# Order edges in the first stage of an attention and mixture kernel, one sink transposition per unit, and later splits of the first expert's weights

## The chip, the cores and the metric

The program runs on one core of a Trainium2 chip. The core has a matrix engine (PE, with weight loads listed apart as PEld), a vector engine (DVE), a scalar engine (ACT), a general engine (POOL), and a queue of transfers that the sync engine (SP) issues. Each engine takes its instructions in the order in which the program lists them. The metric is the time of one execution in microseconds on the device; smaller is better.

## The reference, cut to what matters

```
scores = q @ k.T / sqrt(64)           # 4 batches, 8 heads, 768 positions, head 64
keep   = (position < 4) | (0 <= distance < 128)     # 4 sinks and a window of 128
a      = softmax(where(keep, scores, -1e9));  x = (a @ v) as [3072, 512]
h      = max(x @ w1, x @ w2, x @ w3);  x = h @ w_out          # first mixture, ff 768
order the 3072*8 gate logits, fill 8 experts with 384 tokens each
out[tokens of e] = relu(x[tokens] @ u1[e]) @ u2[e]            # second mixture, ff 1024
```

## The kernel before

The tokens are cut into eight groups of 384 (half a sequence each). The attention of a group is four units, one per pair of heads, 32 units in all, counted by `u['n']`. A unit is loaded (`load`), prepared (`prep`), scored (`score`: six products into banks of the pool `pss`, which has three, copied and masked into the tile T by DVE and ACT), put through the softmax (`soft`: maximum `m` on DVE, six exponentials on ACT with their sums in `l`, the reciprocal on DVE, and the multiplication of T on POOL, line 154) and multiplied with the values (`pv`). In `pv` PE transposes T: three transpositions of blocks of 128 columns into the bank `pt`, of which only the eight rows of the four sinks of two heads are kept, and three for each head into the bank `pp`. ACT and DVE copy the sink rows from `pt` as a high and a low part into the tile `psb` (lines 160 and 161), which meets the sinks' values (tile `vk`, written on POOL in lines 108 and 109) in one product per head, line 177 or 190. The first eight units and units 10 and 11 use the values as they were loaded ("native"); the others split all operands into a high and a low part.

The result of unit p of a group is x_p, a quarter of the contraction of the first mixture. `group` multiplies it with the three weights (line 293, twelve products to a bank of the pool `mm`, which has two banks), so a bank can only be finished when all four units of its group have delivered. The first group's results go straight into a high and a low part (`split`, lines 28 and 29).

The weights of the first mixture arrive as 64-bit words. `single` loads a block (line 228; a ring of four places in the tile HL), takes bits from the second words into a bank of `pss` on DVE (line 235), scales the first words on ACT (line 236), joins both on DVE (line 237) and adds on POOL (line 238). Then a copy on ACT (line 220) and a difference on POOL (line 221) make the high and low parts. A ring place is free for the next load after the addition.

The order of all this up to the last group is worked out when the program is built, by a scheduler that runs a timeline of its own and takes instructions by priority; each engine then follows its list. An edge added by hand (`add_manual_dep`) fixes the order of two instructions without a semaphore where both stand on one engine.

After the last group the tokens are given to experts round by round (lines 418 to 549, mostly on DVE with short counting products on PE), while PE multiplies the last groups with w_out (`x2`, line 318, and `by_rows`, line 350). In the last call of `x2` each bank is copied by ACT (line 320) and split twice (`keep`: ACT line 324, DVE line 325). The experts follow (`expert`): per expert eight blocks f of u1 and u2 are loaded (lines 561 and 562, three places each), split by `weights` (ACT line 566, then DVE or POOL line 567, six places) and multiplied (lines 622 and 615).

Of the kernel before, what the change touches and what calls it, by code (L numbers as in the profile page):

```python
# [21 lines left out]
NEG=-8.0e9  # L22
# [2 lines left out]
    nc.tensor.transpose(out,x,f32(ident))  # L25

def split(nc,hl,x):
    nc.scalar.activation(hl[0],x,AF.Copy)
    nc.vector.tensor_tensor(hl[1],x,f32(hl[0]),op=OP.subtract)

class Attn:
    def __init__(s, tc, q,k,v,vs, keep, consts, pst, psp, pss, psv, work):
        s.tc=tc; s.nc=nc=tc.nc; s.q,s.k,s.v,s.vs=q,k,v,vs
        s.pst,s.psp,s.pss,s.psv,s.w=pst,psp,pss,psv,work
        jp=work.tile([128,128],I32,name="jp",tag="qs0",bufs=2)
        nc.gpsimd.iota(jp,pattern=[[1,128]],base=0,channel_multiplier=-1)
        s.ident=keep.tile([128,128],FR,name="ident")
        nc.vector.tensor_scalar(s.ident,jp,0.0,None,op0=OP.is_equal)
        s.ca=consts.tile([128,2,128],U8,name="ca")
        nc.vector.tensor_scalar(s.ca[:,0,:],jp,0.0,None,op0=OP.is_le)  # L40
        nc.vector.tensor_scalar(s.ca[:,1,:],jp,0.0,None,op0=OP.is_gt)
        s.ul=consts.tile([128,2,128],BF,name="ul")
        nc.vector.tensor_scalar(s.ul[:,0,:],jp,0.0,None,op0=OP.is_lt)
# [10 lines left out]
        s.behind=None; s.n=0; s.no=('kh0','kh1')  # L54
# [9 lines left out]
    def load(s,b,hf,p,native=False):  # L64
        nc=s.nc; w=s.w
        nb=3+hf; S=768; D=64
        u=dict(b=b,hf=hf,p=p,nb=nb,n=s.n,nat=native); s.n+=1
        i=(b*2+hf)*4+p
        half=[(slice(64*h,64*h+64),slice(64-64*h,128-64*h)) for h in range(2)]

        if native:
            u['KK']=s.kf[u['n']%len(s.kf)] if u['n']<8 else s.zeros([s.two(u,[128,4,132],FT,f"kh{h}") for h in range(2)])
            for h,(a,o) in enumerate(half): nc.sync.dma_start(u['KK'][h][a,:nb],s.k[i,a,:nb*132].rearrange("d (c j) -> d c j",j=132))
            u['QF']=w.tile([128,384],FT,name="qf",tag="qs0",bufs=2)
            nc.sync.dma_start(u['QF'],s.q[i])
            u['vn']=w.tile([128,4,2,64],FT,name="vnn",tag="vsp")
        else:
            u['kn']=w.tile([128,4,132],FT,name="kn",bufs=1)
            ld=[nc.sync.dma_start(u['kn'][:,:nb],s.k[i,:,:nb*132].rearrange("p (c j) -> p c j",j=132))]
            u['qn']=[w.tile([128,384],FT,name=f"qn{h}",bufs=1) for h in range(2)]  # L80
            ld+=[nc.sync.dma_start(u['qn'][h][r],s.q[i,a]) for h,(a,o) in enumerate(half) for r in (a,o)]
            if s.behind is not None:
                for x in ld: s.tc.add_manual_dep(x.ins,s.behind.ins.name,mybir.DependencyInfo(mybir.DependencyClass.NoSync,mybir.DependencyReason.DATA),reason="order of loads")
                s.behind=None
            u['vn']=w.tile([128,4,2,64],FT,name="vn",bufs=1)
        nc.sync.dma_start(u['vn'][:,:nb],s.v[i].rearrange("t (c h d) -> t c h d",h=2,d=64)[:,:nb])
        u['sv']=w.tile([40,2,64],FT,name="vns",bufs=1)
        nc.sync.dma_start(u['sv'],s.vs[b*4+p].rearrange("r (h d) -> r h d",h=2))
        return u
    def prep(s,u):  # L90
# [16 lines left out]
        hi,lo=(bass.AP(tensor=VK.tensor,offset=VK.offset+o,ap=[[VK.ap[0][0],40],[st,2],[1,64]]) for o,st in (((0,64),(128,64)) if nat else ((0,192),(64,64))))  # L107
# [37 lines left out]
    def soft(s,u):  # L145
        nc=s.nc; w=s.w; T=u['T']
        m=w.tile([128,6],FT,name="m"); l=w.tile([128,6],FT,name="l")
        nc.vector.tensor_reduce(m,T,axis=AX.X,op=OP.max)
        nc.scalar.activation(m,m,AF.Copy,scale=-0.125)
        for j in range(6):  # L150
            nc.scalar.activation(T[:,j,:],T[:,j,:],AF.Exp,scale=0.125,bias=m[:,j:j+1],accum_out=l[:,j:j+1])
        nc.scalar.activation(l,l,AF.Copy,bias=1e-9)
        nc.vector.reciprocal(l,l)  # L153
        nc.gpsimd.tensor_tensor(T,T,l[:,:,None].to_broadcast([128,6,132]),op=OP.mult)  # L154
    def pv(s,u,x):
        nc=s.nc; w=s.w; T=u['T'].rearrange('p u j -> p (u j)'); hf=u['hf']; nb=u['nb']; nat=u['nat']
        psk=s.pst.tile([128,512],FT,name="pt")
        for i in range(3): flip(nc,psk[:,i*128:(i+1)*128],T[:,264*i+128:264*i+256],s.ident)
        PB=s.pb[u['n']%2]
        nc.scalar.activation(PB[0:8],psk[0:8,:384],AF.Copy)  # L160
        nc.vector.tensor_tensor(PB[32:40],psk[0:8,:384],f32(PB[0:8]),op=OP.subtract)
        jobs=[]
        if hf: jobs.append((0,128,0,0))
        for i in range(3): jobs.append((i*256+128,256 if i<2 else 128,i*128,i+hf))
        for h in range(2):
# [8 lines left out]
            if nat:  # L174
                if h==0:
                    po=s.psv.tile([128,512],FT,name="po")
                    for a_ in range(2): nc.tensor.matmul(po[:,:384],u['VK'][:,a_,:],PB,start=(a_==0),stop=False,skip_group_check=True)
                for c,n,q,blk in jobs:
                    nc.tensor.matmul(po[a,q:q+n],u['vn'][:,blk,h,:],Af[:,c:c+n],start=False,stop=True,skip_group_check=True)  # L179
                if h==1:  # L180
                    for c in x: split(nc,c,po[:,:384]) if type(c) is tuple else nc.scalar.activation(c,po[:,:384],AF.Copy)
# [29 lines left out]
class Moe1:  # L211
# [10 lines left out]
    def single(s,src,ring=False):  # L222

        nc=s.nc
# [9 lines left out]
        s.n+=1  # L234
        nc.vector.tensor_scalar(A,st[:,:,1],0x07ffffff,3,op0=OP.bitwise_and,op1=OP.logical_shift_left)
        nc.scalar.activation(C,st[:,:,0].bitcast(U32),AF.Copy,scale=2.0**-29)
# [70 lines left out]
    def x2(s,H,t0,LG,x2d,n=260,pool=None,keep=None):  # L307

        nc=s.nc; main=s.main; mms=[]
        for t in range(3):  # L310
            o=pool.tile([128,512],FT,name="xq",bufs=4) if pool else s.room(t).tile([128,520],FT,name="xo",bufs=1)
            for u in range(2):
# [6 lines left out]
                with s.tc.high_priority():  # L319
                    nc.scalar.activation(o[:,u*n:(u+1)*n],ps[:,0:n],AF.Copy)  # L320
                    if keep is not None:
                        for d in (2*u,2*u+1):
                            h,l=keep(t,d); c=ps[:,(d-2*u)*128:(d-2*u)*128+128]
                            nc.scalar.activation(h,c,AF.Copy)
# [227 lines left out]
class Moe2:  # L552
# [5 lines left out]
    def weights(s,ev,f):  # L558
# [79 lines left out]
def attention_mixtures(tc,q,k,v,vs,words,wg,u1,u2,out,off=60,spread=(0,1,3,4),native=8,order='a0 a0 a0 a0 w a1 w a1 w a1 w a1 w w a2',order1='a2 o o o o o o a2 a2',back=1,at=(1,0),s1=300,s2=400,nring=6):  # L638
    nc=tc.nc
    PS=bass.MemoryType.PSUM  # L640
    with ExitStack() as ctx:
# [116 lines left out]
def layout(np, i):  # L758
# [12 lines left out]
    vs = np.zeros((4, 4, 40, 2, 64), v.dtype)  # L771
    for h in range(2):
        for r in range(2):
            vs[:, :, 32*r+4*h:32*r+4*h+4, h] = v[:, :, h, :4]
# [30 lines left out]
```

## Time and profile before

| | |
|---|---|
| median of three timed runs | 972.17 us (970.58 to 973.03) |
| the profiled execution, its own time | 963.85 us |
| its span, first to last instruction | 962.1 us |
| mean granted clock of TensorE | 0.992 |
| PE busy | 926.6 us of the span |

The profile shows one execution. Its own time is 1.75 us above its span. The differences that matter for a change are read inside its span and then set against the median of the timed runs, which is 8.3 us above it. A row of a timeline gives the start in us from the span's start, the busy time, the engine, the line, what is written from what, and in brackets the idle time of the engine just before, with what released it. Neighbouring equal rows are merged with their count (x3).

### The profile page before, as it was taken

To read this page: it belongs to the slowest core of one execution; us is meant where nothing else is said; L and a number is where in the kernel's file an instruction comes from. 1 tells how busy PE (TensorE), PEld (TensorE's weight loads), DVE (VectorE), ACT (ScalarE), POOL (GpSimd) and SP (SyncE) were. 2 spreads that over 40 slices of the span, in tenths; PEclk is the share of its full clock that TensorE was granted. 3 is DMA by queue.
4 is the path that set the end of the run, shared out by engine and by line. 5 is a ranking of instruction groups with operands and counts; after the bars stand their busy time and mean duration, and the time that the engine had idled before them with its cause. 6 is when DMAs were issued, how large, how long until landed. Compare 5 with 4: busy or idle time off the path is not lost.

```text
span 962.1 us, 18532 instructions
## 1 busy us (share of the span) xinstructions
PE 926.6 (96%) x6552; PEld 848.2 (88%) x6552; DVE 712.3 (74%) x1855; ACT 489.4 (51%) x1341; POOL 263.8 (27%) x271
## 2 busy tenths in 40 slices
PE   5899999999999999999999999999999999999996
PEld 4679899979989999999999998888888888888895
DVE  6777887677998997886755445888989889874320
ACT  4477554776777876685653211334434434344431
POOL 3687535131232222221311000011103022054321
PEclk8999999999999999999999999999999999999999
DMA  7465321331212222122210002544345353454420
GB/s 212 134 217 165 105 79 62 106 123 49 69 58 90 66 71 71 56 66 80 66 53 2 1 1 88 184 152 132 111 155 176 100 168 119 151 194 164 136 68 33
DMA packets 54444, 99.36 MB, mean 103 GB/s; under 512 B 7792, under 2 KB 24688, under 8 KB 54352
## 3 DMA queue, kind: packets, MB, share of 16 engines
q1 hardware_dynamic: 44464, 75.90, 25.5%
q0 software_dynamic: 3840, 12.45, 3.6%
q10 hardware_dynamic: 6048, 9.83, 2.8%
q8 instruction: 51, 0.84, 0.3%
q14 instruction: 41, 0.34, 0.1%
HBM read 82.17 MB, written 16.12 MB: 102 GB/s over the span
## 4 chain that ended last, share of the span: by engine, by line
PE 73%; DVE 11%; issue 6%; DMA 4%; ACT 3%; POOL 2%; POOLq 0%; SPq 0%; DVEq 0%; ACTq 0%
PE mm L293 25%; PE mm L622 12%; PE acc L615 12%; PE mm L318 6%; PE rc L420 3%; PE po L189 3%; PE ps L130 2%; PE pt L25 2%; PE po L179 2%; DVE kh_w L102 2%; PE pp L25 1%; DMA qf<-in_q_dram 1%; DVE L L185 1%; PE acc L350 1%; PE ps L132 1%
## 5 line engine op out<-in xcount | busy, mean ns | idle before, releaser
L615 PE MATMUL acc<-wbh,HL 128*128 128x512 f32 x384 | 133.1, 401 | 0.0
L318 PE MATMUL mm<-woh,HL 128*128 128x260 f32 (+1 forms) x432 | 88.2, 292 | 5.1 <-ACT xo L320 3.9
L296 DVE TENSOR_TENSOR hm<-mm,hm 128x384 f32<-128x384 f32 x96 | 53.1, 554 | 53.1 <-PE mm L293 48.0
L566 ACT ACTIVATE wah<-sa 128x512 fp32r<-128x512 f32 x64 | 40.5, 632 | 83.5 <-PE mm L622 68.1
L615 PEld LDWEIGHTS acc<-wbh,HL 128*128 128x128 f32 x384 | 71.4, 188 | 12.6 <-ACT HL L625 0.4
L318 PEld LDWEIGHTS mm<-woh,HL 128*128 128x128 f32 x432 | 69.5, 190 | 8.4 <-ACT xo L320 4.8
L566 ACT ACTIVATE wbh<-sb 128x512 fp32r<-128x512 f32 x64 | 40.4, 631 | 71.4 <-PE acc L615 68.7
L615 PE MATMUL acc<-wbl,HL 128*128 128x512 f32 x192 | 76.5, 398 | 0.0
L634 POOL DMA_INDIRECT out_dram<-og,idx x24 | 29.2, 1218 | 169.1 <-ACT og L633 166.3
L293 PE MATMUL mm<-xh,w1h 128*128 128x384 f32 x192 | 66.6, 347 | 1.4 <-ACT w1h L220 0.5
L622 PE MATMUL mm<-HL,wah 128*128 128x384 f32 x256 | 67.4, 341 | 0.0
L293 PE MATMUL mm<-xh,w0h 128*128 128x384 f32 x192 | 66.1, 344 | 0.9 <-DVE hm L296 0.7
L293 PE MATMUL mm<-xh,w2h 128*128 128x384 f32 x192 | 66.4, 346 | 0.0
L293 PE MATMUL mm<-xh,w0l 128*128 128x384 f32 x192 | 65.1, 339 | 0.4 <-POOL w0l L221 0.4
L567 DVE TENSOR_TENSOR wbl<-sb,wbh 128x512 fp32r<-128x512 f32 x64 | 45.2, 706 | 27.1 <-ACT wbh L566 26.8
L293 PE MATMUL mm<-xh,w2l 128*128 128x384 f32 x192 | 65.2, 340 | 0.0
L293 PE MATMUL mm<-xl,w2h 128*128 128x384 f32 x192 | 64.9, 338 | 0.0
L293 PE MATMUL mm<-xh,w1l 128*128 128x384 f32 x192 | 64.9, 338 | 0.0
L293 PE MATMUL mm<-xl,w0h 128*128 128x384 f32 x192 | 64.8, 338 | 0.0
L293 PE MATMUL mm<-xl,w1h 128*128 128x384 f32 x192 | 64.8, 338 | 0.0
L626 DVE SCALAR_TENSOR_TENSOR HL<-mm,HL 128x384 fp32r<-128x384 f32 x64 | 35.5, 555 | 37.8 <-ACT HL L625 37.6
L154 POOL TENSOR_TENSOR T_w<-T_w,l 128x792 f32<-128x792 f32 x22 | 34.2, 1552 | 106.6 <-DVE l L153 106.5
(331 smaller groups left out, 2829.3 us busy)
## 6 DMA issues: line engine op xcount, KB each, us to landing
sa<-in_u_dram SPq DMA_DIRECT2D x64, 256.0 KB
sb<-in_u_dram SPq DMA_DIRECT2D x64, 256.0 KB
HL<-in_words_dram SPq DMA_DIRECT2D x18, 512.0 KB
qn<-in_q_dram SPq DMA_DIRECT2D x88, 96.0 KB
x2d<-xo ACTq DMA_DIRECT2D x15, 256.0 KB
kn<-in_k_dram SPq DMA_DIRECT2D x12, 264.0 KB
st<-in_words_dram SPq DMA_DIRECT2D x6, 512.0 KB
vn<-in_v_dram SPq DMA_DIRECT2D x12, 256.0 KB
```

Of the source, the lines that this page charges most:

```text
L25: nc.tensor.transpose(out,x,f32(ident))
L154: nc.gpsimd.tensor_tensor(T,T,l[:,:,None].to_broadcast([128,6,132]),op=OP.mult)
L189: nc.tensor.matmul(po[:,q:q+n],u['VS'][:,blk,128*h:128*h+128],part[:,c:c+n],start=(part is H and j==0),stop=False,skip_group_check=True)
L293: nc.tensor.matmul(ps[:,:384],s.W[i][a][:,p,f*128:(f+1)*128],X[p][b],start=(n==0),stop=(n==11)); n+=1
L296: else: nc.vector.tensor_tensor(m,ps[:,:384],m,op=OP.max)
L318: mms.append(nc.tensor.matmul(ps[:,:n],H[f][a][:,t*128:(t+1)*128],s.WO[b][:,f,u,c],start=(k==0),stop=(k==17))); k+=1
L566: nc.scalar.activation(h,src,AF.Copy)
L567: (nc.gpsimd if s.n>=6 and nm=="wa" else nc.vector).tensor_tensor(l,src,f32(h),op=OP.subtract)
L615: s.mms.append(nc.tensor.matmul(acc[t],H[f][a][:,t*128:(t+1)*128],W[f][1][b],start=(f==0 and n==0),stop=(f==F-1 and n==2))); n+=1
L622: s.mms.append(nc.tensor.matmul(ps[:,:384],W[f][0][a][:,k,:],X[k][b],start=(n==0),stop=(n==11))); n+=1
L626: nc.vector.scalar_tensor_tensor(l,ps[:,:384],0.0,f32(h),op0=OP.max,op1=OP.subtract)
L634: st=nc.gpsimd.indirect_dma_start(out=s.out,out_offset=bass.IndirectOffsetOnAxis(ap=idx[:,t:t+1],axis=0),in_=o,in_offset=None)
```

## The change

`follow(tc,i,j)` places instruction i behind instruction j. In the first stage it puts the first two scalings of weight words (line 236) behind the softmax sums of unit 0, the next two behind the last exponential of unit 1, and the first DVE steps of three blocks behind the maxima of units 1 and 2; it puts the split of x_0 behind the sums of unit 2, and the clearing of unit 3's T behind the multiplication of unit 1. The DVE product of the first three blocks goes to a bank of `mm` in place of one of `pss`. From unit 8 on, POOL copies the 24 sink columns of T into a small tile S, PE transposes that once, ACT and DVE copy 24 rows of 128 columns where they copied eight rows of 384, and POOL spreads them over `psb` with a mask; the tile of the sinks' values gets 56 rows in place of 40. In the second mixture the splits of blocks f = 4 and above of the first expert are placed on ACT behind the last split of `x2`.

```diff
+def follow(tc,i,j):
+    tc.add_manual_dep(i.ins,j.ins.name,mybir.DependencyInfo(mybir.DependencyClass.NoSync,mybir.DependencyReason.DATA),reason="order on an engine")
...
+        jq=work.tile([128,3],I32,name="jq",tag="m",bufs=2)
+        nc.gpsimd.iota(jq,pattern=[[-8,3]],base=0,channel_multiplier=1)
+        nc.vector.tensor_scalar(jq,jq,-40,None,op0=OP.bitwise_and)
+        s.sm=consts.tile([128,3],FT,name="sm"); nc.vector.tensor_scalar(s.sm,jq,0.0,None,op0=OP.is_equal)
+        s.us=consts.tile([128,128],FR,name="us"); nc.vector.memset(f32(s.us),0.0)
...
-        u['sv']=w.tile([40,2,64],FT,name="vns",bufs=1)
+        u['sv']=w.tile([56,2,64],FT,name="vns",bufs=1)
...
-        if hf==0: nc.gpsimd.memset(T[:,0:2,:],NEG)
+        if hf==0:
+            z=nc.gpsimd.memset(T[:,0:2,:],NEG)
+            if u['n']==3: follow(s.tc,z,s.ev['s',1])
...
+        z=s.ev['l',u['n']]=nc.scalar.activation(l,l,AF.Copy,bias=1e-9)
+        if u['n']==2: follow(s.tc,s.ev['x',0],z)
...
+        if u['n']>=8:
+            S=u["S"]=w.tile([128,24],FT,name="S",bufs=1)
+            nc.gpsimd.tensor_copy(S.rearrange("p (i e) -> p i e",e=8),T.rearrange('p (i v) j -> p i (v j)',v=2)[:,:,128:136])
...
+            U=s.us
+            flip(nc,psk[0:24,0:128],u['S'],s.ident)
+            nc.scalar.activation(U[0:24],psk[0:24,:128],AF.Copy)
+            nc.vector.tensor_tensor(U[32:56],psk[0:24,:128],f32(U[0:24]),op=OP.subtract)
+            nc.gpsimd.tensor_tensor(PB[0:56].rearrange("r (i q) -> r i q",q=128),f32(U)[0:56,None,:].to_broadcast([56,3,128]),s.sm[0:56,:,None].to_broadcast([56,3,128]),op=OP.mult)
...
-        A=s.pss.tile([128,512],FT,name="ps").bitcast(I32); C=st[:,:,0]
+        A=(s.mm.tile([128,512],FT,name="mm") if ring and s.n<3 else s.pss.tile([128,512],FT,name="ps")).bitcast(I32); C=st[:,:,0]
...
+        if n<4: follow(s.tc,z,s.ev['l',0] if n<2 else s.ev['e',1])
+        if n<3: follow(s.tc,y,s.ev['m',1 if n<1 else 2])
...
-            nc.scalar.activation(h,src,AF.Copy)
+            z=nc.scalar.activation(h,src,AF.Copy)
+            if s.n==0 and f>=4: follow(s.tc,z,s.final)
```

## Rows read from the trace of the kernel before

**Rows 1.** The page: busy time of each engine, share of the span, instructions.
```profile
PE 926.6 (96%) x6552; PEld 848.2 (88%) x6552; DVE 712.3 (74%) x1855; ACT 489.4 (51%) x1341; POOL 263.8 (27%) x271
```

**Rows 2.** Stretches of the span: start:end, length, busy us (count) per engine, clock, DMA.
```profile
0.00:20.00 20.00, 10.80 (x39) 7.57 (x40) 13.45 (x53) 6.78 (x24) 8.27 (x21) 0.97 0.75 223
...
20.00:40.00 20.00, 16.01 (x77) 10.61 (x76) 15.62 (x36) 9.27 (x37) 8.85 (x12) 0.86 0.37 105
...
40.00:60.00 20.00, 18.10 (x94) 13.80 (x93) 15.77 (x33) 15.82 (x56) 16.65 (x16) 1.00 0.59 195
...
300.00:400.00 100.00, 99.13 (x676) 98.06 (x676) 88.10 (x166) 70.62 (x224) 26.23 (x29) 1.00 0.24 68
```

**Rows 3.** Timeline of ACT, 12 to 28 us: start, busy us, instruction, [idle before <-releaser].
```profile
12.38 0.66 ACT L236 ACTIVATE HL<-HL 128x512 int32<-128x512 uint32 x1 [9.87 <-DMA HL<-in_words_dram]
...
16.76 0.65 ACT L236 ACTIVATE HL<-HL 128x512 int32<-128x512 uint32 x1 [1.09 <-DMA HL<-in_words_dram]
...
17.31 0.19 ACT L152 ACTIVATE l<-l 128x6 f32<-128x6 f32 x1
...
27.46 0.49 ACT L28 ACTIVATE xh<-po 128x384 fp32r<-128x384 f32 x1 [2.08 <-PE po L179]
```

**Rows 4.** Timeline of PE, the first 50 us.
```profile
4.76 4.55 PE L130 MATMUL ps<-woh,qf 128*128 128x132 f32 x14 [4.76 <-POOL wol L57]
...
18.25 0.68 PE L130 MATMUL ps<-wol,qf 128*128 128x260 f32 x2 [2.41 <-DVE wol L142]
...
22.34 2.09 PE L130 MATMUL ps<-woh,qf 128*128 128x132 f32 x6 [1.43 <-DMA qf<-in_q_dram]
...
49.83 0.55 PE L25 MATMUL pp<-ident,T_w 128*128 128x128 f32 x3 [1.86 <-DVE A_w L170]
```

**Rows 5.** Timeline of POOL near 25 us.
```profile
25.19 0.32 POOL L121 MEMSET T_w<- 128x264 f32 x1 [5.88 <-PE pp L25]
```

**Rows 6.** Timeline of DVE, 30 to 56 us.
```profile
30.18 0.69 DVE L235 TENSOR_SCALAR ps<-HL 128x512 int32<-128x512 int32 x1
...
37.73 0.97 DVE L148 TENSOR_REDUCE m<-T_w 128x6 f32<-128x792 f32 x1
...
55.70 0.56 DVE L29 TENSOR_TENSOR xl<-po,xh 128x384 fp32r<-128x384 f32 x1 [0.41 <-ACT xh L28]
```

**Rows 7.** The stretch from 20 to 25 us, columns as in rows 2.
```profile
20.00:25.00 5.00, 3.57 (x15) 2.90 (x14) 2.67 (x5) 4.91 (x25) 0.00 (x0) 0.50 0.56 132
```

**Rows 8.** Timeline of PE at 57 us: two sets of three transpositions.
```profile
57.12 0.49 PE L25 MATMUL pt<-ident,T_w 128*128 128x128 f32 x3
57.44 0.49 PE L25 MATMUL pp<-ident,T_w 128*128 128x128 f32 x3
```

**Rows 9.** Timeline of ACT, DVE and PE, 625 to 646 us.
```profile
625.61 0.63 ACT L566 ACTIVATE wah<-sa 128x512 fp32r<-128x512 f32 x1 [2.26 <-DMA sa<-in_u_dram]
...
626.15 0.26 ACT L324 ACTIVATE HL<-mm 128x128 fp32r<-128x128 f32 x1
...
626.44 0.29 DVE L325 TENSOR_TENSOR HL<-mm,HL 128x128 fp32r<-128x128 f32 x1 [2.02 <-ACT HL L324]
...
626.79 0.39 PE L318 MATMUL mm<-woh,hh 128*128 128x256 f32 x1 [1.78 <-DVE HL L325]
...
645.91 0.42 PE L622 MATMUL mm<-xh,wah 128*128 128x384 f32 x1
```

**Rows 10.** Timeline of one later unit, 256 to 265 us, all engines.
```profile
256.27 0.48 ACT L160 ACTIVATE psb<-pt 8x384 fp32r<-8x384 f32 x1
...
258.16 0.28 POOL L108 CAST vk<-vns 40x128 fp32r<-40x128 f32 x1 [5.64 <-PE po L190]
...
259.18 0.55 DVE L161 TENSOR_TENSOR psb<-pt,psb 8x384 fp32r<-8x384 f32 x1
...
260.37 1.02 POOL L116 TENSOR_TENSOR vsp<-vn,vsp 128x384 fp32r<-128x384 f32 x1 [1.93 <-ACT vsp L115]
...
264.82 0.39 PE L190 MATMUL po<-psb,vk 128*128 128x384 f32 x1
```

**Rows 11.** Line 102 on DVE: count, shortest/median/longest ns, first and last start.
```profile
L102 DVE TENSOR_TENSOR kh_w<-kn,kh_w x24: 565/704/4530, 95.4 to 436.2; 64x396 fp32r<-64x396 f32 x12, 64x528 fp32r<-64x528 f32 x12
```

More of the change, by code (lines that the diff above doesn't have):

```diff
@@ L27, in split @@
 def split(nc,hl,x):
-    nc.scalar.activation(hl[0],x,AF.Copy)
+    i=nc.scalar.activation(hl[0],x,AF.Copy)
     nc.vector.tensor_tensor(hl[1],x,f32(hl[0]),op=OP.subtract)
+    return i
+def follow(tc,i,j):
+    tc.add_manual_dep(i.ins,j.ins.name,mybir.DependencyInfo(mybir.DependencyClass.NoSync,mybir.DependencyReason.DATA),reason="order on an engine")
 class Attn:
@@ L53, in __init__ @@
         nc.scalar.activation(t,t,AF.Exp)
-        s.behind=None; s.n=0; s.no=('kh0','kh1')
+        jq=work.tile([128,3],I32,name="jq",tag="m",bufs=2)
[3 more added lines that the diff above has]
+        s.us=consts.tile([128,128],FR,name="us"); nc.vector.memset(f32(s.us),0.0)
+        s.behind=None; s.ev={}; s.n=0; s.no=('kh0','kh1')
         s.extra=None
@@ L106, in prep @@
         VK=u['VK']=s.vk[u['n']%2]
-        hi,lo=(bass.AP(tensor=VK.tensor,offset=VK.offset+o,ap=[[VK.ap[0][0],40],[st,2],[1,64]]) for o,st in (((0,64),(128,64)) if nat else ((0,192),(64,64))))
+        hi,lo=(bass.AP(tensor=VK.tensor,offset=VK.offset+o,ap=[[VK.ap[0][0],56],[st,2],[1,64]]) for o,st in (((0,64),(128,64)) if nat else ((0,192),(64,64))))
         nc.gpsimd.tensor_copy(hi,u['sv'])
@@ L147, in soft @@
         m=w.tile([128,6],FT,name="m"); l=w.tile([128,6],FT,name="l")
[L148 removed]
+        s.ev['m',u['n']]=nc.vector.tensor_reduce(m,T,axis=AX.X,op=OP.max)
         nc.scalar.activation(m,m,AF.Copy,scale=-0.125)
         for j in range(6):
[L151 to L152 removed]
+            s.ev['e',u['n']]=nc.scalar.activation(T[:,j,:],T[:,j,:],AF.Exp,scale=0.125,bias=m[:,j:j+1],accum_out=l[:,j:j+1])
+        z=s.ev['l',u['n']]=nc.scalar.activation(l,l,AF.Copy,bias=1e-9)
+        if u['n']==2: follow(s.tc,s.ev['x',0],z)
         nc.vector.reciprocal(l,l)
[L154 removed]
+        s.ev['s',u['n']]=nc.gpsimd.tensor_tensor(T,T,l[:,:,None].to_broadcast([128,6,132]),op=OP.mult)
+        if u['n']>=8:
+            S=u["S"]=w.tile([128,24],FT,name="S",bufs=1)
+            nc.gpsimd.tensor_copy(S.rearrange("p (i e) -> p i e",e=8),T.rearrange('p (i v) j -> p i (v j)',v=2)[:,:,128:136])
     def pv(s,u,x):
@@ L157, in pv @@
         psk=s.pst.tile([128,512],FT,name="pt")
-        for i in range(3): flip(nc,psk[:,i*128:(i+1)*128],T[:,264*i+128:264*i+256],s.ident)
         PB=s.pb[u['n']%2]
-        nc.scalar.activation(PB[0:8],psk[0:8,:384],AF.Copy)
-        nc.vector.tensor_tensor(PB[32:40],psk[0:8,:384],f32(PB[0:8]),op=OP.subtract)
+        if u['n']<8:
+            for i in range(3): flip(nc,psk[:,i*128:(i+1)*128],T[:,264*i+128:264*i+256],s.ident)
+            nc.scalar.activation(PB[0:8],psk[0:8,:384],AF.Copy)
+            nc.vector.tensor_tensor(PB[32:40],psk[0:8,:384],f32(PB[0:8]),op=OP.subtract)
+        else:
+            U=s.us
[3 more added lines that the diff above has]
+            nc.gpsimd.tensor_tensor(PB[0:56].rearrange("r (i q) -> r i q",q=128),f32(U)[0:56,None,:].to_broadcast([56,3,128]),s.sm[0:56,:,None].to_broadcast([56,3,128]),op=OP.mult)
         jobs=[]
@@ L180, in pv @@
                 if h==1:
-                    for c in x: split(nc,c,po[:,:384]) if type(c) is tuple else nc.scalar.activation(c,po[:,:384],AF.Copy)
+                    for c in x: s.ev['x',u['n']]=split(nc,c,po[:,:384]) if type(c) is tuple else nc.scalar.activation(c,po[:,:384],AF.Copy)
                 continue
@@ L230, in single @@
         else: s.tc.add_manual_dep(ld.ins,s.loads[-6].ins.name,mybir.DependencyInfo(mybir.DependencyClass.NoSync,mybir.DependencyReason.DATA),reason="order of loads")
-        A=s.pss.tile([128,512],FT,name="ps").bitcast(I32); C=st[:,:,0]
+        A=(s.mm.tile([128,512],FT,name="mm") if ring and s.n<3 else s.pss.tile([128,512],FT,name="ps")).bitcast(I32); C=st[:,:,0]
         if ring and s.n%3==2: R=s.stage[:,4096:4608]
         else: R=s.conv.tile([128,512],I32,name="cA",bufs=2)
-        s.n+=1
-        nc.vector.tensor_scalar(A,st[:,:,1],0x07ffffff,3,op0=OP.bitwise_and,op1=OP.logical_shift_left)
-        nc.scalar.activation(C,st[:,:,0].bitcast(U32),AF.Copy,scale=2.0**-29)
+        n=s.n; s.n+=1
+        y=nc.vector.tensor_scalar(A,st[:,:,1],0x07ffffff,3,op0=OP.bitwise_and,op1=OP.logical_shift_left)
+        z=nc.scalar.activation(C,st[:,:,0].bitcast(U32),AF.Copy,scale=2.0**-29)
+        if n<4: follow(s.tc,z,s.ev['l',0] if n<2 else s.ev['e',1])
+        if n<3: follow(s.tc,y,s.ev['m',1 if n<1 else 2])
         nc.vector.scalar_tensor_tensor(R,st[:,:,1],-0x40000000,A,op0=OP.bitwise_and,op1=OP.bitwise_or)
@@ L323, in x2 @@
                             h,l=keep(t,d); c=ps[:,(d-2*u)*128:(d-2*u)*128+128]
-                            nc.scalar.activation(h,c,AF.Copy)
+                            s.final=nc.scalar.activation(h,c,AF.Copy)
                             nc.vector.tensor_tensor(l,c,f32(h),op=OP.subtract)
@@ L650, in attention_mixtures @@
         M=Moe1(tc,words,wg,consts,wpool,main,conv,mm,pst,pss,A.ident)
-        M.at=at
+        M.at=at; M.ev=A.ev
         LG=consts.tile([128,24,8],FT,name="LG")
@@ L742, in attention_mixtures @@
         hp.release()
+        E.final=M.final
         trn(0)
@@ L769, in layout @@
         vt[:, hf, :, :, :nb] = v[:, :, :, t].reshape(4, 4, 2, nb, 128, 64).transpose(0, 1, 4, 3, 2, 5).reshape(4, 4, 128, nb, 128)
-    vs = np.zeros((4, 4, 40, 2, 64), v.dtype)
+    vs = np.zeros((4, 4, 56, 2, 64), v.dtype)
     for h in range(2):
         for r in range(2):
-            vs[:, :, 32*r+4*h:32*r+4*h+4, h] = v[:, :, h, :4]
+            for b in range(3): vs[:, :, 32*r+8*b+4*h:32*r+8*b+4*h+4, h] = v[:, :, h, :4]
     w = np.stack([np.asarray(i[f'moe_w{n}']).reshape(4, 128, 6, 128) for n in (1, 2, 3)])
```

2 lines of the change are left out of this document (1 added, 1 removed).

## The prediction

> **What bounds the kernel now.** I read the page's busy times first [rows 1]. PE is busy 926.6 us of a span of 962.1; DVE is next with 712.3. Then I cut the span into stretches [rows 2]. From 300 to 400 us PE works 99.13 of 100 us, and this is how the middle looks: a product taken from PE's list there shortens the whole, and work on another engine costs nothing unless it comes late for PE. The first 60 us are different: PE works 10.80, 16.01 and 18.10 us of three times 20, so it stands still for 60 - 44.91 = 15.1 us, nearly half of all its idle time (962.1 - 926.6 = 35.5). Last I read the timelines of each engine in that first stage [rows 3 to 6] and around the last call of x2 [rows 9]: who stands in front of whom.
>
> In the first stage a product of group 0 cannot end before x_3 is there. Its last part is written by DVE at 55.70 + 0.56 = 56.3 us [rows 6]. Before that PE has two banks for products and then only attention. So what sets the stage is the chain of units 0 to 3 through ACT, POOL and DVE, and each of these has a place where something late stands in front of something ready. On ACT the scaling of weight block 0 waits 9.87 us for its load and starts at 12.38, and block 1 waits until 16.76; the sums of unit 0 stand behind it and come at 17.31 [rows 3]. DVE's reciprocal, POOL's multiplication and PE's first transpositions all wait for these sums; the last scores of unit 2 wait 2.41 us on DVE for the same reason [rows 4]. On POOL the clearing of unit 3's T waits 5.88 us for PE's transpositions of unit 0 and runs at 25.19 [rows 5]; unit 1's multiplication stands behind it. On ACT the split of x_0 waits 2.08 us until 27.46 [rows 3] and holds unit 2's sums. On DVE the first step of weight block 0 runs at 30.18, long after its load, since its bank comes from the three that the scores use; unit 3's maximum comes only at 37.73 [rows 6].
>
> **The change part by part.** *Order edges and banks.* They remove no instruction; they let what is ready go first. PE's first product at 4.76 [rows 4] stays, and so does the wait of 1.43 us for the query load at 22.34 [rows 4], since the loads before it are the same. So of the 15.1 us at most 15.1 - 4.76 - 1.43 = 8.9 us can be won. To this comes the clock. From 20 to 25 us the granted clock is 0.50, the lower level (1.2 GHz), after the idle 2.41 us at 18.25; PE is busy 3.57 us there [rows 7], which at 2.4 GHz would be about half: 1.8 us more, so 10.7 us above. A second bound comes from DVE: between 20 and 60 us it works 15.62 + 15.77 of 40 us [rows 2] and is idle 8.6. If it did the same work without a gap, x_3 would come 8.6 us sooner, at 47.7. Below, the bound is nothing: if unit 3 stays as late, all else only waits for it.
>
> How much of this is reached? Unit 0's sums: the maximum is ready when the scaling takes ACT at 12.38; without that and the second scaling's stay (idle 1.09 us and 0.65 us of work [rows 3]) they come some 2.5 to 3.7 us sooner. The upper end is my estimate from six exponentials started as soon as unit 0's maximum is there. Unit 1's multiplication no longer stands behind the clearing, and unit 2's sums no longer behind x_0. The weight steps of DVE move from 30 us and later into its gaps before 22 us. Unit 3's scores keep their start at 22.34, but its maximum can follow these directly, some 5 us after them, where it now comes 15 us after (37.73). From there to x_3 the chain takes 56.3 - 37.7 = 18.6 us as it is, so x_3 would be at about 46, beyond the DVE bound; DVE will be the limit. Between 0 and 8.6 to 10.7, I take 6.0: nearer the top, as four separate stalls go, but below it, since POOL, DVE and ACT will queue for one another when their gaps are closed. What is late next: unit 3's query load, then DVE's queue.
>
> The edges have a price: the first scalings now run behind exponentials. Block 0's addition on POOL waits for it, and behind this the ring place and the next load. But the addition also needs DVE's two steps, of which the first ran at 30.18 [rows 6], 17 us after the scaling [rows 3]; even with both moved, the scaling comes at some 14 us, behind unit 0's sums, and DVE's first step behind unit 1's maximum, so later. I cost it at nothing; without that cover it would be the scaling's 0.66 us, once. The banks of `mm` are empty until the first product of group 0, so they cost nothing either. The mask needs one more small POOL instruction ahead of PE's first product at 4.76; the trace has nothing closer than the 0.28 us of a small cast [rows 10], so between 0 and 0.28 us; I take 0.2. DVE's new small instructions lie in the gap before that product.
>
> *One transposition per unit.* Units 8 to 31, 24 of them, give up two transpositions each. Three take 57.44 - 57.12 = 0.32 us in PE's stream [rows 8], so one takes 0.107 us, and 48 take 5.1 us. PE is nearly never idle there, so I count all of it. Bounds: 2.5 us, if half of them sit next to waits that then grow; 5.1 us above. In their place ACT copies 128 columns, for which the nearest row has 0.26 us [rows 9], and no longer 384 in 0.48 us [rows 10]; DVE 0.29 [rows 9] for 0.55 [rows 10]. That is 24 x 0.22 = 5.3 us less on ACT and 24 x 0.26 = 6.2 us less on DVE, both hidden behind PE: nothing. POOL gets two more instructions: the copy of 24 columns (at most the 0.28 us of the cast) and the spreading over 384 columns, nearest to the 1.02 us of L116 [rows 10]. That is 1.3 us a unit, 31 us in all on an engine that works 26.23 of 100 us there [rows 2]. The path from the transposition to the sinks' product gets longer by 1.3 - 0.22 - 0.26 = 0.8 us. What hides it: `psb` is ready at 259.18 + 0.55 = 259.7 us and its product runs at 264.82 [rows 10], 5.1 us later. So nothing, with a bound of 0.8 us for each of 24 units, 19 us, if that cover is gone. The taller tiles of the sinks' values keep their columns: nothing.
>
> More work on POOL can also hold DVE. Line 102, which reads two tiles in SBUF, takes 565 ns at its shortest and 4530 at its longest [rows 11]. The Trainium skill's page "SBUF — State Buffer", section "Who interferes with whom", speaks against the change here: a DVE instruction with two SBUF inputs and a POOL instruction that reads SBUF exclude each other for a whole instruction. By that rule the trace agrees: something held line 102 for 4 us, and its inputs can't have, since the time is inside the instruction. In the stretch from 300 to 400 us DVE has 88.10 us of work [rows 2]. With about six units in it (24 over some 400 us), 6 x 1.3 = 7.8 us of blocking at worst, less the 6 x 0.26 = 1.6 us saved, give 94.3 us: still under PE's 99.13. So I cost it at nothing and keep it as a rival.
>
> *Splits behind x2.* On ACT a split for block f = 4 stands at 625.61 after an idle 2.26 us for its load; the second split of x2's bank stands behind it at 626.15, DVE's part waits 2.02 us for that, and PE 1.78 us for DVE [rows 9]. With the edge this split of x2 starts as soon as its bank is full, and PE's 1.78 us go. Bounds: 0, if another wait takes its place, and 1.8. I take 1.8, as a bank then comes free before PE has filled the other one. What is moved: two copies each of f = 4 and f = 5, four of 0.63 us on ACT and as many on DVE, to behind x2; later loads into their three places wait with them. The first product of the expert runs at 645.91 [rows 9], that of f = 4 only after four blocks more, so there is cover.
>
> **The sum.** 6.0 + 5.1 + 1.8 - 0.2 = 12.7 us less. Against the profiled execution's own time: 963.85 - 12.7 = 951.2 us. The median of the timed runs is 8.3 us above that execution; I take the same saving from it: 972.17 - 12.7 = 959.5 us.
>
> **The rivals.** (a) *The first stage keeps its length.* Unit 3 waits for its query load anyway [rows 4], and DVE, at 78% between 20 and 60 us [rows 2], passes the stall on. For it: DVE's list is long. Against it: unit 3's maximum at 37.73 is far behind its scores. Then 5.1 + 1.8 remain, less 0.2 and with up to 2 us from the stage: 972.17 - 6.7 to 8.7, about 964.5. (b) *The transpositions were hidden*, or their place is taken by other waits in PE's stream: 6.0 + 1.8 - 0.2 + 2.5 = 10 at best, 7.6 at worst: 962 to 964.6. Against it: 99.13% busy. (c) *The sinks' product comes late* (the other side). In each of 24 units PE reaches line 177 or 190 before POOL has spread `psb`, because POOL does one thing after the other and the spreading can stand behind a multiplication. It decides when PE waits over 12.7 / 24 = 0.53 us in every unit; at 1 us a unit the time is 972.17 - 12.7 + 24 = 983.5. Against it: the 5.1 us of cover. (d) *POOL holds DVE and DVE holds PE*: 31.2 - 6.2 = 25 us, all of which reaches PE: 984.5. Against it, 94.3 of 100 us. The rule of the Trainium skill's page "SBUF — State Buffer", section "Who interferes with whom", would come out like this at its worst. (e) *The lists are rearranged and nothing is won in sum*: one edge shifts priorities through the first stage, new stalls take what the old ones gave back: 970 to 973.
>
> **How the numbers follow.** What a measurement of this kernel can tell from no change is about 0.3%, 2.9 us. The forecast has a chance of 0.61, (a) 0.17, (b) 0.08, (e) 0.07, (c) 0.04, (d) 0.03. The first three are faster: 0.86. Same is (e), 0.07; slower (c) and (d), 0.07. The range takes the forecast's bounds, 972.17 - (10.7 + 5.1 + 1.8) = 954.6 below, and reaches over (a) and (b) to 968 above: 954 to 968. It leaves out (c), (d), (e) and little of the rest.
>
> **What would show it.** In the trace after: unit 0's sums near 14 us and not 17.31; unit 1's multiplication near 20 us; unit 3's maximum before 31 us; x_3's low part at 48 to 52 us; PE's idle time in the first 60 us at 8 to 10 us; 48 transpositions fewer, 24 x 2; no wait of PE on DVE line 325. Wrong would be: a wait of PE on POOL's spreading, a growth of DVE's two-tile instructions to several us, or an x_3 that still comes at 56 us.

## The result and the profile after

The change made the kernel slower: 980.51 us median (977.25 to 983.00, six runs) against 972.47 (970.58 to 973.03), a ratio of 1.0088 with a 95% interval of 1.0072 to 1.0105. I had forecast 959.5.

The profiled execution of the changed kernel took 979.54 us with a span of 977.8. The kernel before was profiled again during the experiments and had a span of 968.9 there; the profile that the prediction was made on (962.1) came out 6.8 us shorter, all of it in the experts (last section). So the comparison below is with the second one where the experts matter.

The page's busy times, which answer to [rows 1]:

```profile
PE 927.6 (95%) x6504; PEld 846.0 (87%) x6504; DVE 710.3 (73%) x1858; ACT 483.1 (49%) x1341; POOL 293.4 (30%) x320
```

The 48 transpositions are gone (6552 to 6504), ACT has 6.3 us less to do and POOL 30 us more, about as worked out; DVE has only 2.0 us less where 6.2 were worked out. But PE is as busy as before, and its idle time has grown from 35.5 us (40.8 in the second profile) to 50.2. The stretches of [rows 2], in the changed kernel:

```profile
0.00:20.00 20.00, 10.78 (x42) 7.40 (x42) 15.14 (x59) 8.67 (x32) 9.63 (x23) 1.00 0.76 234
20.00:40.00 20.00, 18.32 (x90) 13.59 (x91) 15.63 (x36) 12.07 (x44) 11.52 (x14) 0.91 0.46 150
40.00:60.00 20.00, 18.74 (x98) 14.81 (x97) 17.44 (x36) 12.69 (x46) 14.32 (x13) 1.00 0.56 170
300.00:400.00 100.00, 95.20 (x630) 92.98 (x629) 83.54 (x155) 65.68 (x210) 31.34 (x38) 0.98 0.22 67
```

The first 60 us hold 47.84 us of PE's work in place of 44.91: the first stage did get shorter. From 300 to 400 us PE works 95.20 us where it worked 99.13, at a lower mean clock (0.98). The gain is thrown away in the middle. The places of the first products show where. Group 0 starts at 28.93 us (36.14 in the first profile of before, -7.2), group 1 at 114.1 (-2.4), group 2 at 225.2 (+8.1), the last product of the last group at 591.3 (+7.0). So units 8 to 31, the ones that gave up two transpositions each, run in a stage that is 9.4 us longer.

What PE waited for from 115 to 590 us, first in the second profile of before, then in the changed kernel (line; us in total, times, longest):

```profile
PE mm L318 <- ACT xo L320: 3.9, 3, 1.6
PE po L189 <- DVE x L192: 1.1, 3, 0.5
PE mm L293 <- DVE hm L296: 1.0, 1, 1.0
```

```profile
PE mm L342 <- ACT xo L344: 4.0, 3, 1.7
PE ps L143 <- DVE T_w L153: 3.0, 2, 2.5
PE mm L342 <- DVE HL L362: 2.7, 2, 2.0
PE po L211 <- DVE x L214: 2.7, 3, 2.0
PE mm L317 <- ACT hm L319: 2.0, 3, 1.3
PE ps L143 <- DVE T_w L148: 1.4, 1, 1.4
```

Before, no wait is longer than 1.6 us. Now there are single waits of 2.0 and 2.5 us on DVE. (Line 342 is the product of `x2`, 318 before; 143 the scores of a split unit; 362 the low part of a reloaded group; 153 a mask.) Two of these waits, by the timeline of PE, DVE and POOL from 190 to 209 us:

```profile
190.23 1.30 PE L201 MATMUL po<-A_w,vnn 128*64 128x256 f32 x6
...
191.93 0.70 DVE L111 TENSOR_TENSOR kh_w<-kn,kh_w 64x528 fp32r<-64x528 f32 x1
192.67 0.19 DVE L165 RECIPROCAL l<-l 128x6 f32<-128x6 f32 x1
192.78 0.94 DVE L159 TENSOR_REDUCE m<-T_w 128x6 f32<-128x792 f32 x1
193.63 1.23 DVE L362 TENSOR_TENSOR HL<-hm,HL 128x384 fp32r<-128x384 f32 x1
...
195.85 0.55 DVE L362 TENSOR_TENSOR HL<-hm,HL 128x384 fp32r<-128x384 f32 x1
...
192.94 1.51 POOL L166 TENSOR_TENSOR T_x<-T_x,l 128x792 f32<-128x792 f32 x1 [1.06 <-DVE l L165]
...
194.92 0.51 PE L342 MATMUL mm<-woh,HL 128*128 128x260 f32 x2 [1.98 <-DVE HL L362]
...
196.83 2.35 PE L201 MATMUL po<-A_w,vnn 128*64 128x256 f32 x6
...
200.57 0.82 POOL L183 TENSOR_TENSOR psb<-us,sm 56x384 fp32r<-56x384 f32 x1 [5.64 <-DVE us L182]
201.35 1.28 POOL L125 TENSOR_TENSOR vsp<-vn,vsp 128x512 fp32r<-128x512 f32 x1
...
200.67 2.38 DVE L362 TENSOR_TENSOR HL<-hm,HL 128x384 fp32r<-128x384 f32 x1 [0.18 <-ACT HL L361]
...
207.09 0.39 PE L143 MATMUL ps<-kh_w,qs 128*128 128x260 f32 x1 [2.54 <-DVE T_w L153]
...
207.99 1.30 PE L201 MATMUL po<-A_w,vnn 128*64 128x256 f32 x6
```

Three things are to be seen. On DVE a split of keys, a reciprocal and a maximum stand ahead of the split (line 362) whose result PE needs next: that is the order of a list. That split then takes 1.23 us beside POOL's multiplication of T (line 166, old work). Its next instance, at 195.85 with POOL at rest, takes 0.55, and the one after that 2.38: it runs beside POOL's new spreading (line 183) and the old subtraction behind it (line 125). That is POOL holding DVE, and old work of POOL does it as well as new. And after PE's idle 1.98 us six products take 2.35 us that took 1.30 a little earlier. The stretch shows why:

```profile
196.00:199.00 3.00, 3.00 (x11) 1.70 (x9) 0.80 (x3) 0.59 (x4) 0.00 (x0) 0.50 0.45 124
```

The granted clock is 0.50, the lower level. The changed kernel has three such dips between 190 and 390 us, each behind a wait of 1.4 to 2.0 us; the second profile of before has none between 30 us and the last microseconds. So a wait can cost its own length and then something on top, here 1.05 us in these six products. Not every wait does: after the 2.54 us the same six products take 1.30 us again (207.99).

Three theories fit this: the lists that the scheduler of the build wrote for the changed program are worse (below: rearranged lists); POOL's added work holds DVE or delays the sinks' product; or the edge behind x2 delays the experts.

### The profile page after: what moved, and what is told of

It is laid out like the page before. It is cut to its first block, busy times and chain, and to the rows that moved or that the text cites. A ratio compares the mean times of both kernels' runs of the same rounds, so it can differ in the third digit from the quotient of the medians.

```text
span 977.8 us, 18490 instructions
## 1 busy us (share of the span) xinstructions
PE 927.6 (95%) x6504; PEld 846.0 (87%) x6504; DVE 710.3 (73%) x1858; ACT 483.1 (49%) x1341; POOL 293.4 (30%) x320
## 4 chain that ended last, share of the span: by engine, by line
PE 75%; DVE 11%; ACT 6%; issue 6%; DMA 2%; POOL 0%; SPq 0%; POOLq 0%; another core or an unknown queue 0%; DVEq 0%; ACTq 0%
PE mm L317 24%; PE acc L640 12%; PE mm L647 12%; PE mm L342 7%; PE rc L444 3%; PE po L211 3%; PE po L201 2%; PE ps L141 2%; DMA qf<-in_q_dram 1%; PE pp L25 1%; PE pt L25 1%; PE acc L374 1%; DVE ql L113 1%; DVE kh_w L111 1%; ACT T_w L162 1%
## 5 line engine op out<-in xcount | busy, mean ns | idle before, releaser
L207 DVE TENSOR_TENSOR L<-A_w,H 128x768 fp32r<-128x768 f32 x42 | 45.8, 1090 | 27.0 <-ACT H L206 24.6
```

The costliest lines, as they stand in the source:

```text
L207: nc.vector.tensor_tensor(L,Af,f32(H),op=OP.subtract)
```

## The experiments

Ratios are to the kernel before on the same chip, five rounds each; in brackets the 95% interval. Where a difference of two kernels is given, it is one of medians from one chip, or else of ratios, and then called so.

**One part at a time.** e1 has the edges and banks of the first stage, e2 the single transposition, e3 the edge behind x2, e4 the first and the third.

In e1 and e4 the code of the single transposition is left out, in e1 also the edge of the splits; in e2 all edges and banks; e3 is the kernel before with nothing but

```diff
-            nc.scalar.activation(h,src,AF.Copy)
+            z=nc.scalar.activation(h,src,AF.Copy)
+            if s.n==0 and f>=4: follow(s.tc,z,s.final)
```

e1, expected:

> The kernel before with the order edges and banks of the first stage alone. By the prediction: 6 us less, 966. Theory 1 (the first stage is worth little, and the stage of units 8 to 31 loses whenever its lists come out in another order): PE's first product of group 0 comes some 7 us sooner (29 us), but group 7 starts within 3 us of before, 969 to 975. Theory 2 (the middle loses through the work that the sinks' transposition adds to POOL): the middle keeps all that the first stage wins, so 7 us less here, 965.

e2, expected:

> The kernel before with the single transposition of the sinks in units 8 to 31 alone. By the prediction: 5 us less, 967. Theory 1 (lists): between 970 and 976, with PE's waits spread over many lines. Theory 2 (POOL's added 30 us hold DVE or the sinks' product): 975 to 985, group 7 of the products 5 to 10 us later than before, with the idle time of PE in front of lines 199 and 212 of the sinks' products or on DVE's instructions of two SBUF tiles.

e3, expected:

> The kernel before with the edge behind x2 alone; PE's list differs from that of before only around x2. By the prediction: 1.8 us less, 970.4. Theory 3 (the moved splits come late and hold the loads behind them and DVE's routing work, so that experts 1 to 5 wait): the whole loss of 8.5 us that the changed kernel has from expert 0 on is here, 980, with PE waits of 2 us on the counting's DVE instructions. Rival to 3: the experts' loss comes with the lists of the stage before, then 970 to 973.

e4, expected:

> The changed kernel without the single transposition. If the parts add up, e1 and e3 together: by the prediction 964, by theories 1 and 3 together 978, by theories 2 and 3 together 973, by theory 2 with the rival to 3: 964.

Measured: e1 972.74 against 971.44, ratio 1.0011 (0.9993 to 1.0028); e2 977.74, 1.0075 (1.0050 to 1.0099); e3 970.76, 0.9989 (0.9972 to 1.0006); e4 973.53, 1.0014 (0.9992 to 1.0035). The edge behind x2 is no loss, so theory 3 falls. The first stage alone starts group 0 at 28.7 us in its profile and yet gains nothing at the end. The single transposition carries most of the loss, 6.3 of 8.0 us, although by the working PE has 5 us less to do. But in its trace the order of PE's products up to 590 us differs from that of before in some 2,000 of 3,500 places (the sinks' transpositions left out), so this can't tell the lists from POOL.

**The same instructions in the old order.** The order of each engine's list can be fixed by a chain of the same edges without semaphore that the change uses. e5 is e2 with the lists of all engines as they were before (only the removed transpositions, the smaller copies and POOL's new instructions differ; PE's order in the trace differs in 25 places). e6 is e1 with all lists from 60 us on as before. e7 is the whole change with the lists of before from 60 us on. e8 keeps the old lists and the three transpositions and adds POOL's work alone.

```diff
+def pin(tc,nc,skip):
+    by={}
+    for i in nc.cur_bb.bb.instructions:
+        if i.name not in skip: by.setdefault(str(i.engine).split(".")[1],[]).append(i)
...
+        for a,b in zip(p,p[1:]):
+            tc.add_manual_dep(by[e][b],by[e][a].name,mybir.DependencyInfo(mybir.DependencyClass.NoSync,mybir.DependencyReason.DATA),reason="order on an engine")
```

Here p is the order of one engine's instructions in the list that is kept. e8 adds, in `pv` from unit 8 on and beside the copy into S:

```diff
+            nc.gpsimd.tensor_tensor(s.ud[0:56].rearrange("r (i q) -> r i q",q=128),f32(PB)[0:56,None,0:128].to_broadcast([56,2,128]),s.sm[0:56,0:2,None].to_broadcast([56,2,128]),op=OP.mult)
+            nc.gpsimd.tensor_tensor(s.ud[0:56,0:128],f32(PB)[0:56,0:128],s.sm[0:56,0:1].to_broadcast([56,128]),op=OP.mult)
```

e5, expected:

> The single transposition alone, as in e2, but the lists of all five engines in the stage of attention and groups are pinned to those of the kernel before; only the two removed transpositions and POOL's two new instructions differ. If e2 lost by its rearranged lists: 966 to 968, the 48 transpositions less. If it lost through POOL (the sinks' product late, or DVE held): still 974 to 980. In between, both.

e6, expected:

> The first stage's edges and banks alone, as in e1, but every engine's list from 60 us on is pinned to that of the kernel before. If e1's gain was given back by rearranged lists later: about 965, the 7 us by which group 0 starts sooner less one or two. If what comes after waits for something else anyway (loads of the weights, attention of units 4 to 7): 970 to 972, with group 1's start where it was.

e7, expected:

> All three parts, with the lists pinned as in e5 and e6 (the x2 edge lies behind the pinned stage). If the lists were the cause of the whole loss: e5 and e6 together, 960 to 963, near the prediction on record. If POOL is the cause: 970 or more.

e8, expected:

> The kernel before with all its lists, three transpositions kept, plus POOL's added work alone: in units 8 to 31 the copy of 24 columns and a spreading of 56x384 numbers (in two pieces) into a tile that nobody reads. If POOL's work holds DVE or POOL's queue (theory 2): 976 to 985, DVE's two-tile instructions longer. If it is hidden: 971 to 972.

Measured against 971.16: e5 971.96, 1.0012 (1.0000 to 1.0024); e6 971.95, 1.0008 (0.9993 to 1.0024); e7 966.05, 0.9945 (0.9928 to 0.9963); e8 975.19, 1.0042 (1.0027 to 1.0058).

e7 lies between the two cases named for it, and e8 just below its first. e7 is the changed kernel's own instructions in another order, and it is 0.55% faster than before where the changed kernel is 0.88% slower: by these ratios, which come from two chips, about 14 us between two orders of one program. From 300 to 400 us its PE works 98.33 us, where the changed kernel's works 95.20, and from 115 to 590 us no wait of PE is longer than 1.4 us, where the changed kernel had 2.0 and 2.5:

```profile
300.00:400.00 100.00, 98.33 (x660) 96.26 (x659) 87.40 (x162) 68.49 (x214) 37.45 (x46) 1.00 0.21 62
```

```profile
PE mm L354 <- ACT xo L356: 3.8, 3, 1.4
PE po L223 <- DVE x L226: 3.0, 5, 1.2
PE pt L25 <- POOL S L181: 1.1, 1, 1.1
```

e8 prices POOL's work by itself: 4.0 us. Its DVE rows from 115 to 585 us, and under them those of e3, whose lists there are those of before:

```profile
L213 DVE TENSOR_TENSOR L<-A_w,H 128x768 fp32r<-128x768 f32 x42 | 46.3, 1101 | 16.1 <-ACT H L212 15.6
...
L330 DVE TENSOR_TENSOR HL<-hm,HL 128x384 fp32r<-128x384 f32 x36 | 25.8, 717 | 4.6 <-ACT HL L329 4.3
```

```profile
L193 DVE TENSOR_TENSOR L<-A_w,H 128x768 fp32r<-128x768 f32 x42 | 43.8, 1044 | 16.4 <-ACT H L192 15.7
...
L310 DVE TENSOR_TENSOR HL<-hm,HL 128x384 fp32r<-128x384 f32 x36 | 24.3, 674 | 4.6 <-ACT HL L309 4.4
```

The same work takes DVE 1101 and 717 ns a piece in place of 1044 and 674, and in this stage nothing but POOL's list differs. PE then waits longer for DVE, 2.7 us in place of 1.1 for the low part of x (line 220) and 2.2 in place of 0.9 for a maximum of products (line 324), and for POOL as long as in e3 (0.6 us in both). That is rival (d) at a sixth of its price. In e5 PE also waits for POOL itself (115 to 590 us):

```profile
PE pt L25 <- POOL S L179: 2.1, 3, 1.1
...
PE po L209 <- POOL psb L193: 0.8, 1, 0.8
```

These 2.9 us are waits for POOL's new work; 0.8 of them are rival (c) itself. So in lists held fixed the 5.1 us of transpositions (worked out; no run shows them alone) stand against 4.0 lost through DVE and up to 2.9 on PE's new waits, and e5 comes out where it began. The other 5.5 us of e2's loss are its order.

**Why e6 wins nothing and e7 does.** From 60 us on their lists agree but for the sinks and the splits behind x2. Their first 60 us don't, since the scheduler ordered these anew in each. e10 has e7's lists everywhere, the first stage too, and no single transposition. e9 is the kernel before, profiled again. e11 is e7 with the spreading on ACT:

```diff
-            z=nc.gpsimd.tensor_tensor(PB[0:56].rearrange("r (i q) -> r i q",q=128),f32(U)[0:56,None,:].to_broadcast([56,3,128]),s.sm[0:56,:,None].to_broadcast([56,3,128]),op=OP.mult); s.skip.add(z.ins.name)
+            for i in range(3):
+                z=nc.scalar.activation(PB[0:56,i*128:(i+1)*128],f32(U)[0:56],AF.Copy,scale=s.sm[0:56,i:i+1]); s.skip.add(z.ins.name)
```

e9, expected:

> The kernel before, unchanged, profiled again. All eight profiles of the experiments so far agree in the experts within 1 us and are some 7 us longer there than the profile of before that the prediction was made on. If that profile was an unusual execution: 968 to 972 here, with PE waits of about 1.9 us before the counting products of experts 2 to 5. If the kernel before has shorter experts than all others: 963 to 964.

e10, expected:

> The first stage's edges and the x2 edge without the single transposition, every list of the stage of attention and groups (the first stage too) as in e7. If the first stage is what made e7 faster, and e6 only had a worse list in its first 60 us: e7 less e5's 0.8, about 965, with group 1 some 3 us sooner than before. If e7's gain came from the single transposition: 970 to 972.

e11, expected:

> e7 with the same lists, but the sinks' spreading by three ACT instructions of 56x128 in place of POOL's one of 56x384 in units 8 to 31. If POOL's added work holds DVE and the sinks' product: two thirds of the 4 us of e8 come back, 963. If ACT's queue takes it instead, or POOL's work was hidden in e7: 966 or more.

Measured: e9 970.64 (one run); e10 966.41 against 972.69, 0.9936 (0.9915 to 0.9957); e11 975.46, 1.0034 (1.0017 to 1.0050). e6 came out as its second case says, with group 1 where it was (116.3 us); in e10 group 1 starts at 113.0. So the first stage is worth its gain if the list is right. In e6's first 60 us a scaling of weight words waits 3.75 us on ACT for its load, ahead of the six exponentials of a unit and a weight split; the copies of the scores that PE waits for come last. Its timeline, ACT, DVE and PE:

```profile
48.66 0.68 ACT L258 ACTIVATE HL<-HL 128x512 int32<-128x512 uint32 x1 [3.75 <-DMA HL<-in_words_dram]
...
51.81 0.61 ACT L242 ACTIVATE w1h<-cA 128x512 fp32r<-128x512 f32 x1
52.33 0.58 ACT L159 ACTIVATE wol<-ps 128x132 f32<-128x132 f32 x3
...
52.61 0.70 DVE L160 COPY_PREDICATED wol<-ca,ps 128x128 f32<-128x128 uint8 x3 [3.84 <-ACT wol L159]
...
52.97 0.94 PE L148 MATMUL ps<-woh,qf 128*128 128x260 f32 x2 [2.83 <-DVE wol L160]
```

That is the same kind of stall that the edges took out further ahead; in e10 the exponentials stand first. The profiles of e1 and e4 have a wait of PE of 2.25 and 2.75 us at the same place, those of e7 and e10 none. After it PE in e6 works at a clock of 0.57:

```profile
53.00:57.00 4.00, 4.00 (x13) 3.18 (x14) 3.99 (x11) 2.96 (x8) 3.89 (x4) 0.57 0.31 98
```

e11 went against me: relieving POOL cost nearly 9 us against e7 (by ratios, 1.0034 less 0.9945). DVE is held less (683 ns for the split of a product that takes 776 in e7), but the sinks' product now waits for ACT, twice for up to 3.3 us (115 to 590 us):

```profile
PE po L212 <- ACT psb L196: 6.1, 2, 3.3
```

Behind these two waits PE works at a clock of 0.52 (190.5 to 194 us) and 0.57 (204 to 208 us). So the wait that rival (c) names, a late product of the sinks, is real, but ACT brings it on far more than POOL (0.8 us in e5); POOL, with its idle time, was the better place.

**Whose list it is.** e12 pins PE's list to e7's and leaves the others to the scheduler, e13 DVE's, e14 those of ACT, POOL and SP.

They differ from e7 only in which engines' orders `pin` is given.

e12, expected:

> The changed kernel with PE's list pinned to that of e7, the other engines' left to the planner. If PE's order is the cause: near e7, 966 to 968. If it is DVE's: 974 or more, with PE waits on DVE.

e13, expected:

> The changed kernel with DVE's list alone pinned to that of e7. If DVE's order is the cause: 966 to 968. If PE's is: 974 or more.

e14, expected:

> The changed kernel with the lists of ACT, POOL and SP pinned to those of e7, PE's and DVE's free. If the cause is one engine's list, PE's or DVE's: 974 or more. If any pin of many instructions brings the planner back to the old order: 966 to 970, and the engines can't be told apart in this way.

Measured against 970.65: 974.37, 1.0045 (1.0023 to 1.0067); 974.40, 1.0028 (1.0011 to 1.0045); 975.36, 1.0039 (1.0021 to 1.0056). They give back 0.4, 0.6 and 0.5% of the 1.4% between the changed kernel and e7, where all lists together give back everything. No pin of one part is enough. As the scheduler writes the lists that are not pinned anew, these runs don't show which list carries the loss; that it lies in how the lists fit each other is likely and not shown. Why the scheduler's own timeline preferred them was not tried.

**The parts in good lists, side by side.** e15 is e10 without the edge behind x2; e16 is e10 and e17 is e7 once more.

```diff
-            if s.n==0 and f>=4: follow(s.tc,z,s.final)
```

e15, expected:

> The first stage's edges and banks alone, in the lists of e10. If the first stage carries e10: 965 to 967. If the x2 edge carries a part: 968 or more.

e16, expected:

> e10 once more beside e15 and e17: 0.6 us less than e15 if the x2 edge is worth what e3 gave.

e17, expected:

> e7 once more: within 1 us of e10, if the single transposition wins nothing in sum even where no list changes; 4 to 5 us less, if e5's loss came from elsewhere.

This chip runs the kernel before in 962.85 us. Measured: e15 958.72, 0.9950 (0.9934 to 0.9966); e16 956.20, 0.9928 (0.9914 to 0.9943); e17 956.87, 0.9933 (0.9919 to 0.9947). So the first stage is worth 4.1 us and the edge behind x2 2.5; the single transposition costs 0.7, which these runs can't tell from nothing, since those of e16 and e17 overlap. e16, the first stage and the x2 edge in fixed lists, is the fastest version found, 0.7% below the kernel before, in a tie with e17.

## Why the prediction was wrong, step by step

**The step that failed** is in "One transposition per unit" and under "What bounds the kernel now": "a product taken from PE's list there shortens the whole, and work on another engine costs nothing unless it comes late for PE". This failed twice. POOL's work did come late for PE, through DVE, and took back what the transpositions gave even in fixed lists (e5, e8). And every edit here makes the scheduler write the lists anew, where the working prices one list against the same list: the same program spans 14 us with its order (the changed kernel and e7). My rival (e) named rearranged lists, but only for the first stage, and as a loss no larger than the gain; at 0.07 it was too small.

**The transpositions** (5.1 taken, 2.5 to 5.1 as bounds) came to -0.7 (e17 to e16) and -0.8 (e5). "So I cost it at nothing", for POOL's hold on DVE, was wrong: its work costs 4.0 us through DVE (e8). My comparison, 94.3 of 100 us of DVE's time against PE's 99.13, asked whether DVE would become the bound on average; it was enough that single DVE instructions came late. The Trainium skill's page "SBUF — State Buffer", section "Who interferes with whom", has the rule behind this: a DVE instruction with two inputs in SBUF contends with a POOL instruction that reads SBUF. The trace agrees, with 2.38 us for 0.55 beside POOL's spreading and the subtraction behind it.

**The first stage** (6.0, between 0 and 10.7) measured 4.1 in a good list (e15) and nothing in two others (e1, e6). By the signs that I named, in the changed kernel's timelines of ACT, DVE, POOL and PE, which answer to [rows 3 to 6]:

```profile
13.51 0.21 ACT L163 ACTIVATE l<-l 128x6 f32<-128x6 f32 x1
...
16.54 0.18 DVE L165 RECIPROCAL l<-l 128x6 f32<-128x6 f32 x1
...
20.67 0.19 ACT L163 ACTIVATE l<-l 128x6 f32<-128x6 f32 x1
...
21.63 2.09 PE L141 MATMUL ps<-woh,qf 128*128 128x132 f32 x6 [2.05 <-DMA qf<-in_q_dram]
...
21.83 1.27 POOL L243 TENSOR_TENSOR w0l<-cA,w0h 128x512 fp32r<-128x512 f32 x1 [2.26 <-ACT w0h L242]
23.06 1.50 POOL L166 TENSOR_TENSOR T_w<-T_w,l 128x792 f32<-128x792 f32 x1
...
32.36 0.98 DVE L159 TENSOR_REDUCE m<-T_w 128x6 f32<-128x792 f32 x1
...
50.92 0.56 DVE L29 TENSOR_TENSOR xl<-po,xh 128x384 fp32r<-128x384 f32 x1 [0.20 <-ACT xh L28]
```

Unit 0's sums come at 13.51 us (14 forecast), x_3 at 50.92 (48 to 52): right. But of the 3.8 us by which the sums come sooner only 1.0 reaches what waits for them. DVE's reciprocal runs at 16.54 (17.54 before), since unit 1's maximum and the first weight step, which an edge puts behind that, now stand ahead of it. Unit 1's multiplication comes at 23.06, not 20: its sums come only at 20.67, behind two scalings that an edge puts right behind the last exponential, and on POOL a weight block's difference goes first. Unit 3's maximum comes at 32.36, not before 31. PE's idle time is 60 - 47.84 = 12.2 us and not 8 to 10. That "the loads before it are the same", so that the wait for unit 3's queries stays at 1.43 us, came near: PE is ready for them 1.3 us sooner, they come 0.7 us sooner (21.63), and the wait is 2.05 us, as "What is late next" had said without pricing it. The lower clock that I counted at 1.8 us is still there behind this wait (0.91 from 20 to 40 us, 0.86 before).

**The x2 edge** (1.8, between 0 and 1.8) was right in its wait and near in its size. Side by side it is worth 2.5 us (e15 to e16): PE's wait on the split (1.6 us from 590 to 660 us in e15) is gone in e16, and 1.7 of the 2.5 us lie behind the last product of the groups in the two profiles. In e3 it is worth 0.7 with an interval across nothing. There another wait took its place, as the lower bound says: 0.8 us for a routing step on DVE before the counting products. In the changed kernel, too, there is no wait on the split any more [rows 9], but this one instead:

```profile
640.84 0.77 PE L444 MATMUL rc<-th,ohr 128*128 128x32 bf16 x24 [1.71 <-DVE th L439]
```

**In sum:** where the lists are held, 6.0 us are won (e17) of the 12.7 forecast, and the transpositions, 5.8 below their term, are most of what is missing. With the lists free, the 14 us of the order come on top.

## What to carry to other kernels

Where a scheduler orders the program at build time, an edit's price has two parts, its work and the new order, and here the second (14 us of loss) was over twice the first (6 us of gain); compare the lists first, and hold them fixed to measure the edit. Work moved to POOL, idle as it was, was not free here, since it reads SBUF while DVE does: look at the single late instruction and not at the share of busy time. When PE waits, look at the granted clock of the stretch behind the wait, since part of the wait may be paid again there.

## What the runs showed of the hardware

The spread of one kernel's runs mostly goes with the granted clock: e3's twelve runs go from 968.51 us at a mean clock of 0.998 to 974.40 at 0.991. It does not always: e13 took 970.56 us at 0.993 and 974.40 at 0.994. The six runs of the changed kernel have 0.985 to 0.990, and 29 of the kernel before on one chip 0.988 to 0.996, so a part of the loss goes with a lower clock. That the longer waits bring it about is not shown for every dip: the first profile of before has a clock of 0.51 from 285 to 288.5 us, with no wait of PE over 0.7 us in the 9 us before.

DVE can be held by several POOL instructions in a row. The 4.53 us of line 102 in the kernel before [rows 11] start at 96.05, beside four POOL instructions that follow one another without a gap from 95.77 to 100.15 us. The second profile has the same, with 4.52 us. So one more POOL instruction in such a row can lengthen what DVE waits for.

Chips differ by more than the change does. The kernel before took 970.65 to 972.69 us on four chips and 962.85 on a fifth. The difference lies in the experts. What PE waited for from 660 to 970 us, in the second profile of before:

```profile
PE rc L420 <- DVE th L415: 6.2, 5, 1.8
```

and in the profile that the prediction was made on:

```profile
PE rc L420 <- DVE th L415: 0.2, 1, 0.2
```

The profiles on the fifth chip look like the latter (e16 has 0.2 us there). So 6.8 of the 15.7 us between the two spans that I compared first were not the change's, and what differs between these chips stays open. The 8.3 us between that profile and the median of the timed runs, which the prediction carried along, are of about this size, too; whether they are the same is not shown.
